# Running the first products of a two-layer block three units ahead of the second instead of two

## The chip, the cores and the metric

The kernel runs on one core of one Trainium2 chip. A core has TensorE (PE in the rows; its weight loads are PEld), VectorE (DVE), ScalarE (ACT), GpSimd (POOL) and SyncE (SP), which here only issues DMA. Each engine works through its own queue in order. The metric is device time in microseconds: 930.38 us, the median of three runs from 929.89 to 932.22.

## The reference

Three stages follow each other on 3072 tokens of width 512: attention in chunks of 32 with eight memory keys, a layer of 1024 with a softmax gate and a normalisation, and a last layer of 2048 with a leaky ReLU. The change touches only the last one:

```python
def _moe2_ref(x, w_in, w_out) -> np.ndarray:
    h = x @ w_in
    g = np.maximum(0.01 * h, h)
    return (g @ w_out).astype(np.float32)
```

Here `w_in` (512 x 2048) is W3 and `w_out` (2048 x 512) is W4. Both arrive as 64-bit floats.

## The kernel before

Every product is made from split operands: a value is held as a high and a low half (names ending in h and l, type fp32r), and each product is three matmuls, high by high, high by low, low by high. Raw 64-bit weights are turned into such halves on the chip. `load_raw` (line 92) fetches 128 x 512 of them, 512 KB, with one DMA from the queue of SP into a tile `raw`. `decode_steps` (line 100) then takes one ACT pass (line 107, from `raw` into `m`), four DVE passes (lines 109, 113, 117, 122), an ACT pass that writes the high half (line 129) and a subtraction that writes the low half (line 130; on DVE for W4). The pass of line 122 is the last that reads `raw`.

The tokens go in six blocks of 512. W3 is decoded while the earlier stages run and is parked in memory; `load_w3` (line 474) fetches it back in sixteen pieces, the first eight into `w3a`, the others into `w3b`. W4 is decoded in sixteen pieces during the first block, piece f + 1 being asked for just ahead of unit f.

In each block sixteen units run. `g_unit` (line 512) forms one 128 x 512 piece of the hidden layer: 12 matmuls of line 89 into a PSUM tile `gp` (four buffers), an ACT pass that scales it into `u` (line 518), a DVE maximum (line 519), a cast to the high half `gh` (line 523 on ACT in the first block, line 525 on DVE later) and a subtraction that gives the low half `gl` (line 526, on DVE in the first block, on POOL later). `o_unit` (line 531) multiplies that piece with the matching piece of W4: 12 matmuls of line 535 into four PSUM tiles `po`, three for each of four groups of 128 tokens, in the order gh by w4h, gh by w4l, gl by w4h. The main loop (line 561) puts each finished unit into a list `pend`, and `flush(n)` (line 552) emits `o_unit` for the oldest until n are left. So n says how many units the first products stand ahead of the second.

Just ahead of that loop the second layer's last four column groups are finished: `s_o` (line 338) forms them in the PSUM tile `x2p`, ACT copies each into `x2s` (line 351), which has a single buffer, and a DMA from ACT's queue carries it to `x2d` in memory (line 352). These copies and the first units of the last layer share ACT's queue.

Tiles come from pools that reuse the same memory: `dec2` (line 472) holds `raw` and `m` for W4, `pg` (line 506) holds `u`, `gh` and `gl`. A tile that is put where an older tile lay waits until that one is no longer used. A scheduler orders each engine's queue from the program and gives out the places in the pools.

Of the kernel before, what the change touches and what calls it, by code (L numbers as in the profile page):

```python
# [39 lines left out]
def tile_kernel(  # L40
# [425 lines left out]
    sb, sw3 = ExitStack(), ExitStack()  # L466
# [2 lines left out]
    w3hl = [w3p.tile([P, NF3, 2, KD, P], F32R, name="w3a")]  # L469
    ps_g = sw3.enter_context(tc.tile_pool(name="ps_g", bufs=4, space=PSUM, reuse_waits="tile"))  # L470

    dec2 = sw3.enter_context(tc.tile_pool(name="dec2", bufs=4, side="right", reuse_waits="tile"))

    def load_w3(f):
        w = w3hl[f // NF3][:, f % NF3].bitcast(F32)
        nc.sync.dma_start(out=w.rearrange("p h k f -> p (h k f)"), in_=w3d[f])

    x2e = w3p.tile([P, 2, KD, BT], F32R, name="x2e")
    def load_x(b):
        hl = x2o if b % 2 else x2e  # L480
        h, l = hl[:, 0], hl[:, 1]
        lf = l.bitcast(F32)
        nc.sync.dma_start(out=lf, in_=x2d[b])
        for kk in range(KD):
            nc.scalar.activation(h[:, kk], lf[:, kk], AF.Copy)
            (nc.vector if b < 2 else nc.gpsimd).tensor_tensor(
                out=l[:, kk], in0=lf[:, kk], in1=h[:, kk].bitcast(F32), op=ALU.subtract
            )
        return h, l
# [13 lines left out]
    w3hl.append(w4p.tile([P, KF2 - NF3, 2, KD, P], F32R, name="w3b"))  # L503
    x2o = w4p.tile([P, 2, KD, BT], F32R, name="x2o")
    pb = sb.enter_context(tc.tile_pool(name="pb", bufs=2, reuse_waits="tile"))
    pg = sb.enter_context(tc.tile_pool(name="pg", bufs=3, reuse_waits="tile"))
    ps_o = sb.enter_context(tc.tile_pool(name="ps_o", bufs=1, space=PSUM, reuse_waits="tile"))

    def load_w4(f):
        decode(load_raw(w4[f * P : (f + 1) * P, :], dec2), w4h[:, f], w4l[:, f], dec2, sub=nc.vector)  # L510

    def g_unit(b, f, xh, xl):
        ps = ps_g.tile([P, BT], F32, name="gp")
        w = w3hl[f // NF3][:, f % NF3]
        wh, wl = w[:, 0], w[:, 1]
        mm3(ps, [((wh[:, kk], wl[:, kk]), (xh[:, kk], xl[:, kk])) for kk in range(KD)])
        u = pg.tile([P, BT], F32, name="u")
        nc.scalar.activation(u, ps, AF.Copy, scale=0.01)  # L518
        nc.vector.tensor_tensor(out=u, in0=ps, in1=u, op=ALU.max)  # L519
        gh = pg.tile([P, BT], F32R, name="gh")  # L520
        gl = pg.tile([P, BT], F32R, name="gl")
        if b == 0:
            nc.scalar.activation(gh, u, AF.Copy)  # L523
        else:
            nc.vector.tensor_copy(gh, u)  # L525
        (nc.vector if b == 0 else nc.gpsimd).tensor_tensor(  # L526
            out=gl, in0=u, in1=gh.bitcast(F32), op=ALU.subtract
        )
        return gh, gl

    def o_unit(b, f, gh, gl, po):
        for t in range(TB):
            ts_ = slice(t * P, (t + 1) * P)
            for n, (a, w) in enumerate(((gh, w4h), (gh, w4l), (gl, w4h))):
                nc.tensor.matmul(  # L535
                    po[t], a[:, ts_], w[:, f],
                    start=(f == 0 and n == 0), stop=(f == KF2 - 1 and n == 2),
                )
        if f == KF2 - 1:
            for t in range(TB):  # L540
                late = b == NBLK - 1
                o = pg.tile([P, DM], F32, name="u") if late and t >= 2 else pb.tile([P, DM], F32, name="o")
                od = out[b * BT + t * P : b * BT + (t + 1) * P, :]
                if t % 2:
                    nc.vector.tensor_copy(o, po[t])
                else:
                    nc.scalar.activation(o, po[t], AF.Copy)
                (nc.scalar if late and t % 2 == 0 else nc.sync).dma_start(out=od, in_=o)
# [3 lines left out]
    def flush(n):  # L552
        while len(pend) > n:
            bb, ff, a1, a2 = pend.pop(0)
            if ff == 0:
                po[:] = [ps_o.tile([P, DM], F32, name=f"po{t}") for t in range(TB)]
            o_unit(bb, ff, a1, a2, po)
# [3 lines left out]
    for b in range(NBLK):  # L561
        xh, xl = nx
        for f in range(KF2):
            if b == 0:
                if f + LAG - 1 < KF2:
                    load_w3(f + LAG - 1)
                if f + 1 < KF2:
                    load_w4(f + 1)
            gh, gl = g_unit(b, f, xh, xl)
            pend.append((b, f, gh, gl))  # L570
            flush(2)
            if f == 8 and b + 1 < NBLK:
                nx = load_x(b + 1)
    flush(0)
# [49 lines left out]
```

## Time and profile before

| What | Value |
|---|---|
| Median of three runs | 930.38 us |
| Profiled execution | 930.47 us |
| Its span, first to last instruction | 928.7 us |
| PE busy | 890.5 us, 96% of the span |
| DVE, ACT, POOL busy | 48%, 34%, 19% |
| Mean granted TensorE clock | 0.996 |
| Last layer, start of its first product to the end of its last | 394.62 to 924.99 us |

Times inside the execution are microseconds from the first instruction. The profiled execution lasts 1.77 us longer than its span. The granted clock is a share of full speed: 1.00 is 2.4 GHz, 0.50 is 1.2 GHz.

### The profile page before, as it was taken

How to read it: one execution, taken by the hardware profiler on the slowest of the kernel's cores; microseconds unless marked ns; L12 is line 12 of the kernel's file. 1: busy time of each engine (PE TensorE's matmuls, PEld its weight loads, DVE VectorE, ACT ScalarE, POOL GpSimd, SP SyncE). 2: the span in 40 equal slices, each digit the busy share in tenths (PEclk: the TensorE clock that was granted, in tenths of full speed). 3: DMA queues.
4: the chain of work that ended last, by engine and by line, in shares of the span. 5: the costliest groups of instructions: out<-in, count | busy, mean ns of one | idle time of the engine just before them, and what ended most of it. 6: DMA issues, size and time to landing. Idle time of an engine off the chain costs nothing.

```text
span 928.7 us, 13605 instructions
## 1 busy us (share of the span) xinstructions
PE 890.5 (96%) x5248; PEld 714.8 (77%) x5248; DVE 450.1 (48%) x888; ACT 316.2 (34%) x830; POOL 172.9 (19%) x153
## 2 busy tenths in 40 slices
PE   3789999999999999989999999999999999999998
PEld 2467777777777768868888888888888888888886
DVE  4789976676787778279723112211221132112112
ACT  2477854455555555256421112111211121111111
POOL 2233310000000000000003224222422242222221
PEclk9999999999999999989999999999999999999999
DMA  9656685777888764886111001100200020001001
GB/s 221 170 168 202 183 235 183 223 245 203 253 240 254 209 194 170 329 296 248 45 47 46 1 1 45 46 1 1 80 12 1 1 91 1 0 1 46 1 1 46
DMA packets 51504, 109.94 MB, mean 118 GB/s; under 512 B 6640, under 2 KB 23024, under 8 KB 50672
## 3 DMA queue, kind: packets, MB, share of 16 engines
q1 hardware_dynamic: 38480, 93.87, 32.7%
q10 hardware_dynamic: 12960, 15.21, 5.2%
q8 instruction: 41, 0.67, 0.3%
q14 instruction: 23, 0.19, 0.1%
HBM read 79.70 MB, written 29.36 MB: 117 GB/s over the span
## 4 chain that ended last, share of the span: by engine, by line
PE 82%; DVE 8%; DMA 5%; ACT 2%; POOL 1%; issue 1%; SPq 0%; ACTq 0%; DVEq 0%; POOLq 0%
PE po L535 28%; PE gp L89 28%; PE x2p L345 13%; PE h L89 8%; DMA raw<-in_w 3%; PE att L240 2%; PE att L198 1%; DVE so L284 1%; PE tr L254 1%; ACT p L215 1%; DVE m L122 1%; POOL rstd L292 1%; PE tr L228 1%; DMA x2d<-x2s 1%; DVE hnm L276 1%
## 5 line engine op out<-in xcount | busy, mean ns | idle before, releaser
L519 DVE TENSOR_TENSOR u<-gp,u 128x512 f32<-128x512 f32 x96 | 66.3, 691 | 329.2 <-ACT u L518 329.2
L518 ACT ACTIVATE u<-gp 128x512 f32<-128x512 f32 x96 | 57.4, 598 | 370.5 <-PE gp L89 370.5
L526 POOL TENSOR_TENSOR gl<-u,gh 128x512 fp32r<-128x512 f32 x80 | 103.4, 1292 | 304.1 <-DVE gh L525 290.1
L535 PE MATMUL po<-w4h,gh 128*128 128x512 f32 x384 | 150.3, 391 | 3.3 <-ACT gh L523 3.1
L535 PE MATMUL po<-w4h,gl 128*128 128x512 f32 x384 | 150.5, 392 | 1.3 <-DVE gl L526 1.3
L535 PE MATMUL po<-w4l,gh 128*128 128x512 f32 x384 | 150.1, 391 | 0.0
L345 PE MATMUL x2p<-lhl,w2h 128*128 128x512 f32 x384 | 126.1, 404 | 2.3 <-ACT lhl L333 2.0
L535 PEld LDWEIGHTS po<-w4h,gh 128*128 128x128 f32 x384 | 72.5, 189 | 19.2 <-ACT gh L523 3.6
L535 PEld LDWEIGHTS po<-w4h,gl 128*128 128x128 f32 x384 | 72.6, 189 | 16.8 <-DVE gl L526 1.7
L345 PEld LDWEIGHTS x2p<-lhl,w2h 128*128 128x128 f32 x384 | 70.2, 188 | 19.2 <-ACT lhl L333 2.5
L535 PEld LDWEIGHTS po<-w4l,gh 128*128 128x128 f32 x384 | 72.5, 189 | 15.0
L345 PE MATMUL x2p<-lhl,w2l 128*128 128x512 f32 x192 | 77.7, 404 | 0.0
L89 PE MATMUL h<-w1l,xh 128*128 128x512 f32 x168 | 67.8, 404 | 1.9 <-POOL w1l L130 1.9
L89 PE MATMUL h<-w1h,xh 128*128 128x512 f32 x168 | 69.2, 412 | 0.5 <-ACT w1h L129 0.5
L89 PE MATMUL gp<-x2e,w3a 128*128 128x512 f32 x288 | 69.5, 391 | 0.0
L89 PE MATMUL gp<-x2o,w3a 128*128 128x512 f32 x288 | 69.2, 389 | 0.0
L89 PE MATMUL gp<-x2e,w3b 128*128 128x512 f32 x288 | 69.2, 389 | 0.0
L89 PE MATMUL gp<-x2o,w3b 128*128 128x512 f32 x288 | 69.2, 389 | 0.0
L89 PE MATMUL h<-w1h,xl 128*128 128x512 f32 x168 | 66.9, 398 | 0.0
L215 ACT ACTIVATE p<-att,nms 128x64 f32<-128x64 f32 x192 | 57.4, 320 | 22.8 <-DVE nms L208 22.6
L89 PEld LDWEIGHTS gp<-x2e,w3a 128*128 128x128 f32 x288 | 54.6, 190 | 11.5
L292 POOL TENSOR_TENSOR rstd<-ve,mhalf 128x1 f32<-128x1 f32 x24 | 15.9, 661 | 253.4 <-DVE ve L290 200.7
(107 smaller groups left out, 1259.8 us busy)
## 6 DMA issues: line engine op xcount, KB each, us to landing
raw<-in_w SPq DMA_DIRECT2D x48, 512.0 KB, 5.1
kbd<-in_kw SPq DMA_DIRECT2D x46, 256.0 KB, 4.6
vbd<-in_vw SPq DMA_DIRECT2D x46, 256.0 KB, 4.4
lnd<-sl SPq DMA_DIRECT2D x16, 512.0 KB, 3.8
lt<-lnd ACTq DMA_DIRECT2D x64, 128.0 KB, 4.4
q<-in_qt SPq DMA_DIRECT2D x24, 256.0 KB, 4.8
x2d<-x2s ACTq DMA_DIRECT2D x24, 256.0 KB, 3.9
out<-o SPq DMA_DIRECT2D x21, 256.0 KB, 2.0
```

Of the source, the lines that this page charges most:

```text
L89: nc.tensor.matmul(ps, a, b, start=(i == 0), stop=(i == 3 * n - 1))
L122: nc.vector.scalar_tensor_tensor(out=mu, in0=raw[:, :, 1], scalar=0x80000000, in1=mu, op0=ALU.bitwise_and, op1=ALU.bitwise_or,)
L198: nc.tensor.matmul(sc[cs, 2 * hp : 2 * hp + 2, :], q[:, hp, cs], k[:, :, hp, c, :], start=True, stop=True,)
L215: nc.scalar.activation(p[:, h], sc[:, h], AF.Exp, bias=nms[:, h : h + 1], scale=SCALE, accum_out=rs[:, h : h + 1],)
L228: nc.tensor.transpose(ptp[:, hp], p[:, 2 * hp : 2 * hp + 2].rearrange("p h k -> p (h k)"), ident)
L240: nc.tensor.matmul(xp[cs, 2 * hp : 2 * hp + 2, :], pt[:, hp, cs], v[:, :, hp, c, :], start=True, stop=True,)
L292: nc.gpsimd.tensor_tensor(out=rstd, in0=ve, in1=mhalf, op=ALU.pow)
L345: nc.tensor.matmul(ps, a[:, kk, es], r[:, kk], start=(kk == 0 and n == 0), stop=(kk == KF - 1 and n == 2),)
L518: nc.scalar.activation(u, ps, AF.Copy, scale=0.01)
L519: nc.vector.tensor_tensor(out=u, in0=ps, in1=u, op=ALU.max)
L526: (nc.vector if b == 0 else nc.gpsimd).tensor_tensor(out=gl, in0=u, in1=gh.bitcast(F32), op=ALU.subtract)
L535: nc.tensor.matmul(po[t], a[:, ts_], w[:, f], start=(f == 0 and n == 0), stop=(f == KF2 - 1 and n == 2),)
```

## The change

Three numbers change. `pg` gets four buffers each for `u`, `gh` and `gl` instead of three; `dec2` gets three each for `raw` and `m` instead of four; and the list is flushed down to three units instead of two. A buffer of `u`, `gh` and `gl` together takes 6 KB in each partition, and so does one of `raw` and `m`, so the space in total stays as it is, while the places inside it shift.

```diff
-    dec2 = sw3.enter_context(tc.tile_pool(name="dec2", bufs=4, side="right", reuse_waits="tile"))
+    dec2 = sw3.enter_context(tc.tile_pool(name="dec2", bufs=3, side="right", reuse_waits="tile"))
...
-    pg = sb.enter_context(tc.tile_pool(name="pg", bufs=3, reuse_waits="tile"))
+    pg = sb.enter_context(tc.tile_pool(name="pg", bufs=4, reuse_waits="tile"))
...
             gh, gl = g_unit(b, f, xh, xl)
             pend.append((b, f, gh, gl))
-            flush(2)
+            flush(3)
```

On PE, where the last layer begins (the rows with x2p are the end of the layer before it; `po` is numbered because it has four tiles), the difference reads:

```order
 L345 MATMUL x2p<-lhl,w2l 128x512
-L89 MATMUL gp<-x2e,w3a 128x512 x36
-L535 MATMUL po_4441<-w4h,gh 128x512
-L535 MATMUL po_4441<-w4l,gh 128x512
-L535 MATMUL po_4441<-w4h,gl 128x512
+L89 MATMUL gp<-x2e,w3a 128x512 x48
+L535 MATMUL po_4472<-w4h,gh 128x512
+L535 MATMUL po_4472<-w4l,gh 128x512
+L535 MATMUL po_4472<-w4h,gl 128x512
```

Twelve matmuls of a fourth unit now stand ahead of the first matmul on W4; from there on the two kinds alternate by twelve as they did, one unit further apart.

On DVE, at the same place, the first low half of an activation (line 526) reads in the difference:

```order
 L519 TENSOR_TENSOR u<-gp,u 128x512 [waits Activation_49]
-L526 TENSOR_TENSOR gl<-u,gh 128x512 [waits DMAHW3_49,DMAHW6_49,DMAHW2_49,Activation_49]
+L526 TENSOR_TENSOR gl<-u,gh 128x512 [waits Activation_49]
 L130 TENSOR_TENSOR w4l<-m,w4h 128x512 [waits Activation_49]
 L526 TENSOR_TENSOR gl<-u,gh 128x512 [waits Activation_49]
```

The three waits on DMAs that it loses are those of the transfers from `x2s` to `x2d`: in the kernel before, the first `gl` lies where `x2s` lay, and now the third `gh` does. On ACT's queue, with the tiles' numbers, before the change:

```order
L518 ACTIVATE u_4372<-gp_4359 128x512 [waits PE_49]
L107 ACTIVATE m_4413<-raw_4411 128x512 [waits DMAHW4_49]
L518 ACTIVATE u_4403<-gp_4390 128x512 [waits PE_49]
L523 ACTIVATE gh_4375<-u_4372 128x512 [waits DVE_49]
L129 ACTIVATE w4h_4325<-m_4382 128x512 [waits DVE_49]
L523 ACTIVATE gh_4406<-u_4403 128x512 [waits DVE_49]
L518 ACTIVATE u_4434<-gp_4421 128x512 [waits PE_49]
L107 ACTIVATE m_4460<-raw_4458 128x512 [waits DMAHW6_49,Activation_49]
L523 ACTIVATE gh_4437<-u_4434 128x512 [waits DVE_49]
```

and after it:

```order
L518 ACTIVATE u_4372<-gp_4359 128x512 [waits PE_49]
L107 ACTIVATE m_4413<-raw_4411 128x512 [waits DMAHW4_49,DVE_49]
L518 ACTIVATE u_4403<-gp_4390 128x512 [waits PE_49]
L523 ACTIVATE gh_4375<-u_4372 128x512 [waits DVE_49]
L129 ACTIVATE w4h_4325<-m_4382 128x512 [waits DVE_49]
L523 ACTIVATE gh_4406<-u_4403 128x512 [waits DVE_49,Pool_49]
L518 ACTIVATE u_4434<-gp_4421 128x512 [waits PE_49]
L107 ACTIVATE m_4444<-raw_4442 128x512 [waits DMAHW6_49,Activation_49]
L523 ACTIVATE gh_4437<-u_4434 128x512 [waits DMAHW3_49,DVE_49]
```

The order is the same; the pass on the fourth raw piece (`raw_4411`) also waits for DVE now, and the wait on the last transfer out of `x2s` (DMAHW3) has moved to the third `gh`. On SP's queue, the issues from the third raw piece of W4 on, before the change:

```order
L95 DMA raw_4380<-in_w4 128x1024 [waits DMAHW1_49,Pool_49]
L476 DMA w3a_4186<-w3d_62 128x1024 [waits DMAHW2_49]
L95 DMA raw_4411<-in_w4 128x1024 [waits DMAHW4_49]
L476 DMA w3a_4186<-w3d_62 128x1024 [waits DMAHW5_49]
L95 DMA raw_4458<-in_w4 128x1024 [waits DMAHW6_49,DVE_49,Activation_49]
```

and after it:

```order
L95 DMA raw_4380<-in_w4 128x1024 [waits DMAHW1_49]
L476 DMA w3a_4186<-w3d_62 128x1024 [waits DMAHW2_49]
L95 DMA raw_4411<-in_w4 128x1024 [waits DMAHW4_49,DVE_49,Activation_49]
L476 DMA w3a_4186<-w3d_62 128x1024 [waits DMAHW5_49]
L95 DMA raw_4442<-in_w4 128x1024 [waits DMAHW6_49,DMAHW7_49,DVE_49,Activation_49]
```

The fourth raw piece has no free buffer of its own any more: its issue waits for DVE's pass of line 122 on the first piece, and the issue of a W3 piece stands behind it.

## Rows read from the trace of the kernel before

**Rows 1.** The page, section 1 (busy us, share of the span, instructions)

```profile
PE 890.5 (96%) x5248; PEld 714.8 (77%) x5248; DVE 450.1 (48%) x888; ACT 316.2 (34%) x830; POOL 172.9 (19%) x153
```

**Rows 2.** Chain of waits, around the start and end of the last layer: start, us, what

```profile
394.62 5.46 PE gp L89 x24
...
400.71 6.27 DMA x2d<-x2s
...
407.93 4.63 PE po L535 x10
412.56 3.29 PE gp L89 x12
415.85 2.72 PE po L535 x12
...
916.82 8.17 PE po L535 x36
```

**Rows 3.** Timeline of PE, 394.4 to 408: start, us, what, idle and releaser

```profile
394.45 8.32 PE L89 MATMUL gp<-x2e,w3a 128*128 128x512 f32 x36
405.92 0.50 PE L535 MATMUL po<-w4h,gh 128*128 128x512 f32 x1 [3.14 <-ACT gh L523]
...
407.93 0.80 PE L535 MATMUL po<-w4h,gl 128*128 128x512 f32 x1 [1.28 <-DVE gl L526]
```

**Rows 4.** Stretches: length, busy PE PEld DVE ACT POOL, clock, DMA share, GB/s

```profile
330.00:335.00 5.00, 3.51 (x16) 2.56 (x14) 3.56 (x5) 1.81 (x6) 0.02 (x1) 1.00 0.90 273
...
406.00:407.00 1.00, 0.65 (x2) 0.21 (x2) 0.40 (x1) 1.00 (x3) 0.00 (x0) 0.87 0.98 395
413.00:414.00 1.00, 1.00 (x4) 0.79 (x4) 1.00 (x3) 0.15 (x1) 0.00 (x0) 0.71 0.40 57
424.00:434.00 10.00, 10.00 (x46) 8.29 (x45) 10.00 (x19) 6.83 (x13) 0.00 (x0) 1.00 0.96 383
454.00:464.00 10.00, 10.00 (x46) 8.29 (x45) 4.57 (x8) 3.03 (x5) 0.00 (x0) 1.00 0.00 0
```

**Rows 5.** Timeline of ACT, 394 to 406

```profile
394.50 0.33 ACTq L352 DMA_DIRECT2D x2d<-x2s  x1
...
400.08 0.60 ACT L351 ACTIVATE x2s<-x2p 128x512 f32<-128x512 f32 x1 [3.98 <-PE gp L89]
...
402.70 0.58 ACT L518 ACTIVATE u<-gp 128x512 f32<-128x512 f32 x1
403.17 0.66 ACT L107 ACTIVATE m<-raw 128x512 f32<-128x512 f32 x1
...
405.23 0.63 ACT L523 ACTIVATE gh<-u 128x512 fp32r<-128x512 f32 x1 [0.92 <-DVE u L519]
```

**Rows 6.** Timeline of DVE, 394 to 408

```profile
397.22 0.69 DVE L122 SCALAR_TENSOR_TENSOR m<-raw,m 128x512 uint32<-128x512 uint32 x1
...
404.52 0.68 DVE L519 TENSOR_TENSOR u<-gp,u 128x512 f32<-128x512 f32 x1
...
405.72 0.68 DVE L519 TENSOR_TENSOR u<-gp,u 128x512 f32<-128x512 f32 x1
407.18 0.69 DVE L526 TENSOR_TENSOR gl<-u,gh 128x512 fp32r<-128x512 f32 x1 [0.78 <-ACT gh L523]
```

**Rows 7.** Timeline of SP's queue, 394 to 424: issue, us of issuing, what

```profile
394.17 0.43 SPq L95 DMA_DIRECT2D raw<-in_w  x1
394.65 0.43 SPq L476 DMA_DIRECT2D w3a<-w3d  x1
...
400.99 0.37 SPq L95 DMA_DIRECT2D raw<-in_w  x1
...
420.54 0.33 SPq L95 DMA_DIRECT2D raw<-in_w  x1
```

**Rows 8.** Tile raw, its four issues from 393 to 411: us to landing

```profile
DMA to landing us min/median/max: 3.9/4.5/6.5
```

**Rows 9.** The page, section 6: issues, KB each, median us to landing

```profile
x2d<-x2s ACTq DMA_DIRECT2D x24, 256.0 KB, 3.9
```

## The prediction

> **What bounds the kernel now.** I read the page first: PE is busy for 890.5 of 928.7 us [rows 1], so only a gap of PE, or a stretch in which it runs slowly, can give time back. Next the chain of waits, for the last layer alone. From 412.56 on it is PE and nothing but PE, in pieces of twelve matmuls that take 2.72 us [rows 2]. The layer has 6 blocks of 16 units with two such pieces each, 192 pieces, so PE could do it in 192 x 2.72 = 522.24 us. It starts at 394.62 and ends at 916.82 + 8.17 = 924.99, 530.37 us later [rows 2]. So 8.13 us are lost somewhere. Nearly all of it is at the start: from 394.62 to the end of the sixth piece at 415.85 + 2.72 = 418.57 are 23.95 us, and six pieces are 16.32, which leaves 7.63 us [rows 2]. The other 0.50 us lies later, and I do not touch it.
>
> The timeline of PE shows the first part of the 7.63: after three units of W3 it stops at 402.77 and waits 3.14 us for the first `gh`, does two matmuls, and waits another 1.28 us for the first `gl` [rows 3]. That is 4.42 us. The stretches show the rest: the granted clock, 1.00 before, is 0.87 on average from 406 to 407 and 0.71 from 413 to 414 [rows 4]; ten matmuls from 407.93 take 4.63 us where twelve take 2.72, and the next twelve 3.29 [rows 2]. So PE runs at its lower level of 1.2 GHz for some six microseconds after it has stood idle, and this and the restart make the other 3.21 us.
>
> Last the timelines of the engines that PE waits for. ACT fills `x2s` at 400.08, which has one buffer and so needs the transfer that ACT issued at 394.50; it took until 400.0 [rows 5]. (The row names PE as the releaser, but a product of the next layer frees nothing there.) Behind it on ACT stand the first `u` at 402.70 and the first `gh` at 405.23 [rows 5]. The first `gl` on DVE is later still, at 407.18 [rows 6], because it lies where `x2s` lay and waits for the last transfer, 400.71 + 6.27 = 406.98 [rows 2].
>
> **The change, part by part.**
>
> *A fourth unit ahead.* Twelve matmuls move in front of the first product with W4. They add nothing in sum. PE then has work until 402.77 + 2.72 = 405.49. Its first matmul with W4 wants `gh` there, and the third wants `gl` two matmuls later, at 2 x 2.72 / 12 = 0.45 us more, 405.94.
>
> *The shifted buffers.* The first `gl` no longer waits for the transfer of 400.71. Everything else left as it was, `gh` is done at 405.23 + 0.63 = 405.86 [rows 5]. DVE comes free 0.60 us after it starts the second maximum (its passes of this size start that far apart, 404.52 to 405.72 for two), at 405.72 + 0.60 = 406.32, so `gl` runs from 406.32 to 407.01 [rows 6]. PE would wait 405.92 - 405.49 = 0.43 us and then about 407.05 - 406.37 = 0.68 us: 1.1 us in place of 4.42.
>
> *Three raw buffers.* The fourth raw piece was issued at 394.17. Now its issue waits for DVE's pass of 397.22, and goes out at 397.22 + 0.69, about 398.0 [rows 6], with the W3 piece of 394.65 behind it on SP's queue [rows 7]. This does two things of opposite sign.
>
> First, the transfer from `x2s` at 394.50 loses two rivals of 512 KB each for its first 3.5 us. It took 5.5 us before; the median of its 24 kind is 3.9 [rows 9]. At 3.9 it lands at 398.4, 1.6 us sooner, and the queue of ACT moves up with it: `u` from 402.70 to 401.1, the first maximum on DVE from 404.52 to 402.9. The Trainium skill ("DMA: Bandwidth & Descriptors", section "Issuing engines are not separate DMA queues") says that transfers issued by SP and by ACT run on the same sixteen engines and interleave, whoever issued them. By that rule the transfer gets quicker, as I take it; if ACT's transfers went their own way it would land at 400.0 still, and the 1.1 us above would stay. The trace agrees with the rule, in that 5.5 and 6.27 us were taken while other transfers ran, against a median of 3.9.
>
> Second, ACT's pass on that piece (403.17 before [rows 5]) now has a wait ahead of it, and the second `u` and the first `gh` stand behind it. Landings of `raw` in this stretch took 3.9 to 6.5 us, median 4.5 [rows 8], so the piece is there at 398.0 + 4.5 = 402.5 (401.9 to 404.5). At 402.5 the pass ends at 403.2, the second `u` at 403.7, the first `gh` at about 404.4; on DVE the second maximum runs from 404.1 to 404.8 and `gl` from there to 405.5. Both are ready before PE wants them, at 405.49 and 405.94: no wait, with 0.4 us to spare. At 6.5 everything from the pass on is 2 us later, `gl` ends at about 407.2, and PE waits some 1.2 us. So the cost of this part lies between 0 and 1.2 us at the start; I take 0, as the median landing does.
>
> *The clock.* With no gap, or with one of about 1 us, I expect no fall. From 330 to 335 PE stood idle for 1.49 of 5 us and the clock stayed at 1.00 [rows 4]; it fell after 3.14 and 1.28 us with only two matmuls between. So the 3.21 us go as well.
>
> *Later units.* Each unit now has six pieces, 16.3 us, from the end of its first product to the start of its second instead of four, 10.9 us, so a late `gh` or `gl` is covered better than before. At the end of the kernel three units stand after the last first product instead of two; that is the same work.
>
> **The sum.** The profiled execution took 930.47 us, 0.09 above the median of the three runs. 930.47 - 7.63 = 922.84, and against the median 922.75. I say 922.9.
>
> **Rivals.**
>
> *Part of the wait stays.* The transfer out of `x2s` is no quicker, or the raw piece lands late: 1.1 or 1.2 us as worked out, 924.0; up to about 3 us if both happen, 925.8. For it: DMA engines were busy at 0.96 to 0.98 of their time there [rows 4]. Against it: the later issues leave less in flight from 394 to 398.
>
> *The wait only moves.* If the fourth raw piece lands after about 407, 9 us after its issue, `gh` is as late as before plus one unit, the clock falls again, and the time is 926 to 930.4. Nothing in rows 8 comes near 9 us. That the change doesn't do what it says would give the same, 930.4; the order on PE shows that it does.
>
> *Slower: three raw buffers are too few for the rest of the first block.* One turn of a buffer, from an issue to the next issue into it, took 420.54 - 400.99 = 19.55 us with four buffers [rows 7], one piece each 4.9 us, while PE uses one in 5.44. If a turn stays that long with three, that is 6.5 us a piece. The fourth piece goes out at 398.0 and the sixteenth four turns later; it is decoded a turn after that, at 398.0 + 5 x 19.55 = 495.8. PE wants it at 405.49 + 15 x 5.44 = 487.1. PE then waits 8.7 us in that block, and if these waits bring the clock down once more, 3.2 on top: 922.84 + 11.9 = 934.7. It begins to cost at a turn of (487.1 - 398.0) / 5 = 17.8 us. Against it: the turn was long because DVE had four pieces in hand and worked without a break (10.00 of 10 us from 424 to 434), and it was through by about 459, some 30 us ahead of need (4.57 of 10 us from 454 to 464) [rows 4]; three in hand should turn round in about three quarters of that, 14.7 us. The Trainium skill ("Perfetto Trace Analysis", section "Optimization Strategy") warns that gaps which repeat on the engine that should be full can mean too few buffers for the next tile. It speaks against taking one away, and by it the time would be the one of this rival. The trace shows no repeating gap of PE in the first block with four buffers, and no run here yet with three.
>
> **How the numbers follow.** No wait left: 0.66, with 922.2 to 923.5 as its own range (it may also gain or lose some of the 0.50 us elsewhere). Part stays: 0.20, 923.5 to 926. Wait only moves, or nothing done: 0.08, 926 to 930.4. Slower: 0.06, about 934.7. A measurement of this kernel can tell 0.3%, 2.8 us, from no change, so faster means below 927.6: the first two cases and a third of the third, 0.88. Same 0.07, the rest of the third and the mildest of the fourth; slower 0.05. The range for 8 times in 10 is 922.0 to 926.0.
>
> **What would show it.** Right: 48 matmuls of W3 in one piece from 394.4 to about 405.5, the first product with W4 within 0.5 us behind them, a clock of 1.00 from 402 to 416, and 2.72 us for every piece; the first `x2s` wait on ACT ending near 398.5. Wrong: an idle row of PE above 1 us at 405.5 (with ACT's pass on `raw` waiting for a DMA it is the late landing; with `gl` waiting for `gh` alone it is ACT's queue), any idle of PE with W4 as releaser between 420 and 490, or a clock below 1.00 after 406.

## The result and the profile after

The changed kernel takes 921.13 us, the median of three runs (920.85, 921.13, 923.98), against 930.38 before: a ratio of 0.9908, with a 95% interval from 0.9881 to 0.9936. It is faster, by more than the 7.5 us forecast; 921.13 lies 0.9 us below the lower end of the predicted range. The same kernel run six more times in a later round gave a median of 922.87 and a ratio of 0.9921 (0.9896 to 0.9945). All nine runs together have their median at 922.74.

The profiled execution took 920.85 us with a span of 919.1 us and a mean granted clock of 1.00. Its page begins with this line (busy us, share of the span, instructions), which answers to [rows 1]:

```profile
PE 887.1 (97%) x5248; PEld 713.2 (78%) x5248; DVE 450.9 (49%) x888; ACT 315.8 (34%) x830; POOL 172.8 (19%) x153
```

The chain of waits through the last layer, as in [rows 2] (start, us, what):

```profile
393.10 10.88 PE gp L89 x48
403.98 2.72 PE po L535 x12
406.70 2.72 PE gp L89 x12
...
904.46 10.89 PE po L535 x48
```

The DMA, ACT and DVE pieces of [rows 2] are gone. The layer runs from 393.10 to 904.46 + 10.89 = 915.35, which is 522.25 us, or 192 pieces of 2.72 us: PE has nothing left to lose there. The timeline of PE says the same, with no idle time in front of the first product with W4, against 3.14 and 1.28 us in [rows 3]:

```profile
392.94 11.04 PE L89 MATMUL gp<-x2e,w3a 128*128 128x512 f32 x48
403.82 0.39 PE L535 MATMUL po<-w4h,gh 128*128 128x512 f32 x1
...
404.27 0.39 PE L535 MATMUL po<-w4h,gl 128*128 128x512 f32 x1
```

The stretches of [rows 4], in the trace after (busy PE, PEld, DVE, ACT, POOL; granted clock, DMA share, GB/s):

```profile
406.00:407.00 1.00, 1.00 (x7) 0.80 (x6) 1.00 (x3) 1.00 (x3) 0.00 (x0) 1.00 0.92 369
413.00:414.00 1.00, 1.00 (x6) 0.82 (x5) 1.00 (x3) 0.44 (x1) 0.00 (x0) 1.00 0.89 328
424.00:434.00 10.00, 10.00 (x46) 8.29 (x45) 8.05 (x15) 5.63 (x10) 0.00 (x0) 1.00 0.76 259
454.00:464.00 10.00, 10.00 (x46) 8.29 (x45) 4.62 (x8) 3.67 (x7) 0.00 (x0) 1.00 0.01 2
```

The clock stays at its upper level where it was 0.87 and 0.71, and DVE has slack from 424 to 434 where it had none.

Now the engines that PE waited for. The timelines of ACT, DVE and SP's queue answer to [rows 5 to 7]; subtract 392.94, the layer's start here, to compare with before, where it was 394.45. ACT:

```profile
392.44 0.33 ACTq L352 DMA_DIRECT2D x2d<-x2s  x1
...
396.84 0.60 ACT L351 ACTIVATE x2s<-x2p 128x512 f32<-128x512 f32 x1 [2.80 <-DMA x2d<-x2s]
...
400.80 0.68 ACT L107 ACTIVATE m<-raw 128x512 f32<-128x512 f32 x1 [0.76 <-DVE w4l L130]
401.38 0.57 ACT L518 ACTIVATE u<-gp 128x512 f32<-128x512 f32 x1
402.00 0.63 ACT L523 ACTIVATE gh<-u 128x512 fp32r<-128x512 f32 x1
```

DVE:

```profile
395.15 0.69 DVE L122 SCALAR_TENSOR_TENSOR m<-raw,m 128x512 uint32<-128x512 uint32 x1
...
403.08 0.68 DVE L526 TENSOR_TENSOR gl<-u,gh 128x512 fp32r<-128x512 f32 x1
```

SP's queue:

```profile
395.91 0.33 SPq L95 DMA_DIRECT2D raw<-in_w  x1
...
408.44 0.33 SPq L95 DMA_DIRECT2D raw<-in_w  x1
```

The transfer out of `x2s` that the first copy waits for takes 396.84 - 392.44 = 4.40 us from its issue to the next copy, against 400.08 - 394.50 = 5.58. The fourth raw piece goes out at 395.91, behind DVE's pass of 395.15, and nothing waits for its landing: ACT's pass on it waits 0.76 us for DVE. `gh` is done at 402.63 and `gl` at 403.77, ahead of PE's first matmuls that read them, at 403.82 and 404.27.

So the span became 9.6 us shorter. The layer accounts for 530.37 - 522.25 = 8.1 us. The other 1.5 us is outside: the layer starts at 393.10 on the chain instead of 394.62, in code that the change leaves alone. The chain of waits at the very start shows where that comes from. Before:

```profile
3.02 9.36 DMA raw<-in_w
12.40 13.58 DMA raw<-in_w
```

After:

```profile
3.01 8.45 DMA raw<-in_w
11.48 12.18 DMA raw<-in_w
```

These are two loads of raw weights, 512 KB each, one behind the other. The first is issued at the same moment in both; the second goes out from SP's queue as the first lands, at 12.40 and 11.48. They took 22.94 us together before and 20.63 after. Whether that is the change or the execution was the first question for the experiments.

### The profile page after: what moved, and what is told of

Same layout as the page of the kernel before. It is cut to its first block, busy times and chain, and to the rows that moved or that the text cites. A ratio compares the mean times of both kernels' runs of the same rounds, so it can differ in the third digit from the quotient of the medians.

```text
span 919.1 us, 13605 instructions
## 1 busy us (share of the span) xinstructions
PE 887.1 (97%) x5248; PEld 713.2 (78%) x5248; DVE 450.9 (49%) x888; ACT 315.8 (34%) x830; POOL 172.8 (19%) x153
## 4 chain that ended last, share of the span: by engine, by line
PE 85%; DVE 7%; DMA 3%; ACT 2%; POOL 1%; issue 1%; SPq 0%; ACTq 0%; DVEq 0%; POOLq 0%
PE po L535 28%; PE gp L89 28%; PE x2p L345 14%; PE h L89 9%; DMA raw<-in_w 2%; PE att L240 2%; PE att L198 1%; DVE so L284 1%; PE tr L254 1%; PE tr L228 1%; ACT p L215 1%; POOL rstd L292 1%; DVE hnm L276 1%; DVE m L122 1%; DVE nms L207 1%
## 5 line engine op out<-in xcount | busy, mean ns | idle before, releaser
L89 PEld LDWEIGHTS gp<-x2o,w3b 128*128 128x128 f32 x288 | 54.1, 188 | 11.2
```

Source lines behind the costliest of these rows:

```text
L89: nc.tensor.matmul(ps, a, b, start=(i == 0), stop=(i == 3 * n - 1))
```

## The experiments

Ten runs were made, each with a trace. The table puts these and the two of before and after side by side. S is the start of the first product of the last layer in PE's timeline. "Loads" is the sum of these two DMAs near the head of the program. "Copy" is the time from the issue of the transfer out of `x2s` near S to the next copy into `x2s`. "Idle" is PE's idle time ahead of its first products with W4. "Clock fell" says whether the granted clock fell in the layer. "Lost" is the time from S to the end of the last product, less the 522.4 us that the changed kernel took in its first profile.

| Trace | units ahead | raw buffers | first `gl` on x2s's place | S | loads | copy | idle: `gh`, `gl` | clock fell | lost |
|---|---|---|---|---|---|---|---|---|---|
| before | 2 | 4 | yes | 394.45 | 22.94 | 5.58 | 3.14, 1.28 | yes | 8.1 |
| after | 3 | 3 | no | 392.94 | 20.63 | 4.40 | none | no | 0 |
| e0_again | 3 | 3 | no | 394.74 | 23.05 | 4.66 | 0, 0.29 | no | 0.6 |
| e1_lag2 | 2 | 3 | no | 394.06 | 22.42 | 4.79 | 1.84, 0.40 | yes | 4.5 |
| e2_raw4 | 3 | 4 | no | 396.37 | 23.42 | 5.80 | 1.67, 0.41 | no | 2.8 |
| e3_swap | 3 | 3 | yes | 389.07 | 17.16 | 4.78 | none | no | 0.4 |
| e4_swap_before | 2 | 4 | no | 392.78 | 21.15 | 7.04 | 4.61, 0 | yes | 8.6 |
| e5_dec3 | 2 | 3 | yes | 393.45 | 20.83 | 4.68 | 2.18, 0.40 | yes | 4.7 |
| e6_dec2 | 3 | 2 | no | 392.46 | 20.87 | 3.43 | 1.92, 0 | no | 2.7 |
| e7_swap_b | 3 | 3 | yes | 392.27 | 20.58 | 4.50 | 0, 0.73 | no | 1.3 |
| e8_swap_c | 3 | 3 | yes | 393.61 | 21.29 | 4.61 | 0, 0.54 | no | 0.9 |
| e9_swap_d | 3 | 3 | yes | 393.98 | 22.29 | 4.35 | 0, 0.58 | no | 0.9 |

**The changed kernel once more (e0_again).** No edit.

> The changed kernel once more, to tell the share of the change from what differs between executions. The last layer lost 8.1 us before and 0.0 after, and it began 1.5 us sooner after, in code that the change leaves alone. Theory A (the 1.5 us come from the first loads and differ from run to run): the layer begins anywhere from 392.5 to 395 in this profile, and over five rounds the kernel is 8.1 us faster, a ratio of 0.9913. Theory B (they belong to the change): it begins near 393 again, and the ratio is 0.990 or below.

The median of six runs was 922.87 against 929.92. In this execution the two loads took 23.05 us and the layer began at 394.74, as late as before the change; it took 923.23 us in all. PE waited 0.29 us for `gl`. Four profiles of one kernel, e3_swap and its repeats below, differ more: loads from 17.16 to 22.29 us and starts from 389.07 to 393.98. Over the twelve traces S less the sum of the loads lies between 371.5 and 373.0, while the sum itself runs over 6.3 us. So the start of the layer follows these two DMAs, whatever the kernel is, and the 1.5 us of the first profile were the execution's and not the change's. Why the two loads take so differently long is not shown. The shortest case, from the chain of e3_swap:

```profile
3.02 7.06 DMA raw<-in_w
10.09 10.10 DMA raw<-in_w
```

**The unit ahead alone taken back (e1_lag2).**

```diff
-            flush(3)
+            flush(2)
```

> The changed kernel with the list flushed down to two units again; four buffers for the activation, three raw buffers and all places stay. Measured by what the last layer takes beyond 522.25 us, its 192 pieces of 2.72 (8.1 in the kernel before, 0.0 in the changed one). Theory A (the start-up gap is closed by three parts, the unit ahead being one): counted from the first matmul of the layer, PE runs out at 8.3 us, the first gh was done at 9.7 and the first gl at 10.8 in the changed kernel, so PE waits about 1.4 and 0.4 us and the layer loses 2.2 us with the clock staying at 1.00. Theory B (only the unit ahead counts): the gap of before is back, 7.6 us. Theory C (the unit ahead does nothing, the buffers did it): 0.

Median 926.37 of ten, ratio 0.9970 (0.9949 to 0.9991). The idle rows of PE's timeline:

```profile
404.23 0.50 PE L535 MATMUL po<-w4h,gh 128*128 128x512 f32 x1 [1.84 <-ACT gh L523]
405.36 0.50 PE L535 MATMUL po<-w4h,gl 128*128 128x512 f32 x1 [0.40 <-DVE gl L526]
```

The granted clock fell right behind them, in the stretches of the same trace:

```profile
406.00:407.00 1.00, 1.00 (x4) 0.79 (x3) 1.00 (x3) 0.48 (x1) 0.00 (x0) 0.56 1.04 311
```

Without the fourth unit 4.5 us are lost: 2.24 of idle time, as theory A had it, and the rest with the restart and a fall of the clock that theory A did not expect. By these two traces the smaller pool and the shifted places together give the other 8.1 - 4.5 = 3.6 us.

**Three raw buffers alone, in the kernel before (e5_dec3).**

```diff
-    dec2 = sw3.enter_context(tc.tile_pool(name="dec2", bufs=4, ...
+    dec2 = sw3.enter_context(tc.tile_pool(name="dec2", bufs=3, ...
```

> The kernel before with three raw buffers instead of four and nothing else: two units ahead, and the first gl still lies where x2s lay. Theory A: the fourth raw piece goes out later, the transfer out of x2s lands sooner, ACT's queue moves up 1.6 us; the first gh is ready 9.7 us after the start of the layer, but the first gl waits for the last transfer out of x2s until about 11.2, so PE waits 1.4 and then 1.6 us: 3.3 us lost if the clock stays, some 6 if it falls. Theory B (raw buffers only cost): 7.6 us or more, as before.

Median 926.67 of ten, ratio 0.9959 (0.9937 to 0.9981). The copy into `x2s` comes 4.68 us after the issue instead of 5.58, PE waits 2.18 us for `gh` and 0.40 for `gl`, and 4.7 us are lost:

```profile
403.96 0.50 PE L535 MATMUL po<-w4h,gh 128*128 128x512 f32 x1 [2.18 <-ACT gh L523]
405.09 0.79 PE L535 MATMUL po<-w4h,gl 128*128 128x512 f32 x1 [0.40 <-DVE gl L526]
```

The smaller pool by itself gains 8.1 - 4.7 = 3.4 us by the traces, and the interval of the ten times lies clear of 1. `gl` still lies where `x2s` lay, yet its wait, expected at 1.6 us, is as long as in e1_lag2, where it does not.

**The place of the first `gl` alone, in the kernel before (e4_swap_before).** The pool `pg` is opened ahead of `pb`, so that its tiles fall on other places.

```diff
-    pb = sb.enter_context(tc.tile_pool(name="pb", bufs=2, reuse_waits="tile"))
     pg = sb.enter_context(tc.tile_pool(name="pg", bufs=3, reuse_waits="tile"))
+    pb = sb.enter_context(tc.tile_pool(name="pb", bufs=2, reuse_waits="tile"))
```

> The kernel before with the two pools pg and pb taken in the other order and nothing else, which moves the first gl off the place of x2s (the second unit's gl comes to lie there). Theory A: the first gl runs at 406.3 instead of 407.18 on the clock of the trace before, 0.9 us sooner; the wait for gh (3.1 us) stays and with it the fall of the clock: 6.5 to 7 us lost at the start, and about 4 if the clock does not fall. Theory B (the place of gl is what counted): close to 0.

Median 929.0 of ten, ratio 1.0002 (0.9971 to 1.0033): no gain, to within 0.3%, some 3 us. `gl` no longer waits for the transfer, but `gh` still does, behind the copy on ACT's queue, and in this execution the copy came 7.04 us after the issue, 1.46 us later than before:

```profile
405.71 0.80 PE L535 MATMUL po<-w4h,gh 128*128 128x512 f32 x1 [4.61 <-ACT gh L523]
```

So the 8.6 us lost here do not price the place alone. Less the 1.46 us of the later copy they would be some 7.1, an estimate near theory A's 6.5 to 7.

**The place of `gl` put back in the changed kernel (e3_swap; the same kernel again in e7_swap_b, e8_swap_c and e9_swap_d).** The same swap of the two lines, in the changed kernel.

> The changed kernel with the two pools pg and pb taken in the other order and nothing else, which puts the first gl back where x2s lay. Theory A: with three units ahead and ACT's queue early, gl waits for the last transfer out of x2s only until about 11.1 us after the start of the layer, ends at 11.8, and PE wants it at 11.3: 0.6 us lost, clock 1.00. Theory B (the place of the first gl is the main part): 4 us or more lost.

Median 921.51 of ten (917.4 to 927.12), ratio 0.9923 (0.9893 to 0.9952), the same as e0_again to within the intervals. In its trace PE waits for nothing. Six of its ten runs had a mean clock of 0.996 to 0.999, though, while all nine of the changed kernel had 1.00, so three more profiles were taken of it.

> The kernel of e3_swap once more (the changed kernel with the first gl back on the place of x2s), for a second look at its last layer, since six of its ten executions had a mean granted clock below 1.00 and all nine of the changed kernel had 1.00. If the place of gl costs nothing that matters, the layer again lasts 522.4 to 523.5 us at a clock of 1.00 throughout, and a mean clock below 1.00 comes from a fall before the layer, near 336, as in e2_raw4. If it matters in those executions in which the last transfer out of x2s lands late, gl on DVE starts 11.5 us or more after the layer begins, PE shows an idle row of 0.5 to 2 us with gl as releaser, and the layer lasts 523.5 to 526 us, with the clock falling inside it.

> The same kernel, a third look, with the same two readings: 522.4 to 523.5 us for the layer with any fall of the clock lying before it, or 523.5 to 526 with a row of PE that waits 0.5 to 2 us for gl and the clock falling behind it.

> The same kernel, a fourth look, with the same two readings. If none of the three shows a mean clock below 1.00, the question stays open.

All three show a PE that waits for `gl`, by 0.73, 0.54 and 0.58 us, at a clock of 1.00 throughout; the layer lost 1.3, 0.9 and 0.9 us. From DVE's timeline in e8_swap_c, the transfer is what `gl` waits for:

```profile
404.90 0.69 DVE L526 TENSOR_TENSOR gl<-u,gh 128x512 fp32r<-128x512 f32 x1 [0.33 <-DMA x2d<-x2s]
```

Four traces with `gl` on that place lost 0.4 to 1.3 us, two without it 0 and 0.6. So the place is worth about half a microsecond once the rest of the wait is gone, an estimate from six traces that the times do not resolve. Where the clock fell in the six runs stays open, since none of the four profiled ones shows a fall.

**Four raw buffers kept, with the fourth unit (e2_raw4).** To make room, `u` has two buffers, and `gl` and `gh` are placed ahead of it; the output tile that shares the name `u` gets the same number.

```diff
-        decode(load_raw(w4[f * P : (f + 1) * P, :], dec2), ...
+        raw = dec2.tile([P, 512, 2], U32, name="raw", bufs=4)
+        nc.sync.dma_start(out=raw.rearrange("p f w -> p (f w)"), in_=w4[f * P : (f + 1) * P, :])
+        decode(raw, ...
...
-        u = pg.tile([P, BT], F32, name="u")
+        gl = pg.tile([P, BT], F32R, name="gl")
+        gh = pg.tile([P, BT], F32R, name="gh")
+        u = pg.tile([P, BT], F32, name="u", bufs=2)
...
-        gh = pg.tile([P, BT], F32R, name="gh")
-        gl = pg.tile([P, BT], F32R, name="gl")
```

> The changed kernel (three units ahead, four buffers of gh and gl) with four raw buffers; the room for it comes from u, which has two buffers; m keeps three, the first gl is off the place of x2s and the third gh on it, as in the changed kernel. The fourth raw piece is issued at once again. Theory A (the later issue speeds the transfer out of x2s and with it ACT's queue): ACT's queue is as late as in the kernel before, the first gl ends some 12.6 us after the start of the layer, and PE, which has work until 10.9, loses about 1.1 us, clock at 1.00. Theory B (raw buffers do not matter): 0 lost. Theory C (three raw buffers were a cost that the unit ahead outweighs): 0 lost and the decode ends sooner.

Median 924.73 of ten, ratio 0.9927 (0.9896 to 0.9959), which cannot be told from e0_again. The execution of the trace took 927.03 us, the second longest of the ten; in it 2.8 us are lost:

```profile
409.07 0.50 PE L537 MATMUL po<-w4h,gh 128*128 128x512 f32 x1 [1.67 <-ACT gh L525]
410.21 0.50 PE L537 MATMUL po<-w4h,gl 128*128 128x512 f32 x1 [0.41 <-DVE gl L528]
```

ACT's timeline says why. Two transfers out of `x2s` follow each other on one buffer:

```profile
390.66 0.33 ACTq L352 DMA_DIRECT2D x2d<-x2s  x1
...
396.81 0.60 ACT L351 ACTIVATE x2s<-x2p 128x512 f32<-128x512 f32 x1 [6.18 <-DMA x2d<-x2s]
397.44 0.33 ACTq L352 DMA_DIRECT2D x2d<-x2s  x1
...
403.24 0.60 ACT L351 ACTIVATE x2s<-x2p 128x512 f32<-128x512 f32 x1 [4.20 <-DMA x2d<-x2s]
```

The second is issued 1.07 us after S, where it was 0.05 in the kernel before, and takes 5.80. It is so late because the first went out late, at 390.66 or 5.71 us ahead of S, against 7.55 before; the first took no longer than in the kernel before (396.81 - 390.66 = 6.15 us to the next copy). This is one execution, so its 1.07 cannot be laid on the buffers.

**Two raw buffers (e6_dec2).**

```diff
-    dec2 = sw3.enter_context(tc.tile_pool(name="dec2", bufs=3, ...
+    dec2 = sw3.enter_context(tc.tile_pool(name="dec2", bufs=2, ...
```

> The changed kernel with two raw buffers instead of three, to see how near three are to too few. Turns of a raw buffer took 10 to 13.6 us with three. Theory A (a turn is mostly waiting in DVE's queue and shrinks with the buffers): a turn of about 10 us, 5.0 a piece against the 5.44 that PE uses, so no repeating gap; but ACT's passes on the third and fourth raw piece stand ahead of the first gh and wait for later transfers, which costs about 2 us at the start. Theory B (a turn has a floor of 12 us or more): 6 us a piece, PE waits again and again in the first block, 5 us or more in sum, and the clock may fall.

Median 923.24 of five, ratio 0.9933 (0.9905 to 0.9962). The copy comes soonest of all, after 3.43 us, but now ACT waits for the raw piece, and `gh` stands behind it:

```profile
400.73 0.66 ACT L107 ACTIVATE m<-raw 128x512 f32<-128x512 f32 x1 [1.42 <-DMA raw<-in_w]
404.19 0.66 ACT L107 ACTIVATE m<-raw 128x512 f32<-128x512 f32 x1 [2.81 <-DMA raw<-in_w]
404.76 0.61 ACT L523 ACTIVATE gh<-u 128x512 fp32r<-128x512 f32 x1
```

PE waits for it once:

```profile
405.43 0.50 PE L535 MATMUL po<-w4h,gh 128*128 128x512 f32 x1 [1.92 <-ACT gh L523]
```

That is its only idle row between 405 and 480. Two buffers still keep the whole first block fed.

## Why the prediction was right, and where it was wrong

*What bounds the kernel.* Right. The forecast counted 192 x 2.72 us for the layer and 8.13 us lost; after the change the layer takes 522.25 us and loses nothing.

*A fourth unit ahead.* Right, and the largest term. PE has work for 11.04 us from S, as forecast. Taken back alone (e1_lag2) it costs 4.5 us in the trace, and 3.5 between the medians (926.37 and 922.87).

*Three raw buffers.* Right in mechanism; that the size fits so well is partly luck. Forecast after S and measured: the `x2s` copy at 4.05 and 3.90, `gh` done at 9.95 and 9.69, `gl` at 11.05 and 10.83. But the transfer was to take 3.9 us from an issue at S + 0.05, and took 4.40 from an issue at S - 0.50. In e0_again it went out at S + 0.15 and took 4.66, and where the forecast had 0.4 us to spare PE waited 0.29. In the eight traces with three buffers the copy comes 4.35 to 4.79 us after the issue, against 5.58, 5.80 and 7.04 in the three with four, and 3.43 with two. The Trainium skill ("DMA: Bandwidth & Descriptors", section "Issuing engines are not separate DMA queues") states that transfers issued by different engines share the sixteen engines. The traces agree with it: fewer loads from SP at that moment, and the transfer from ACT is quicker. In the stretch from 1.55 to 3.55 us after S the share of the DMA engines' time that was busy fell from 0.93 to 0.47; before the change:

```profile
396.00:398.00 2.00, 2.00 (x10) 1.65 (x10) 1.90 (x4) 0.10 (x1) 0.00 (x0) 1.00 0.93 338
```

and after it:

```profile
394.50:396.50 2.00, 2.00 (x10) 1.66 (x9) 1.93 (x4) 0.00 (x0) 0.00 (x0) 1.00 0.47 180
```

What the smaller pool is worth is shown without the fourth unit (e5_dec3); beside it, it rests on the one trace of e2_raw4, since the times do not part the two kernels. The wait that was feared, ACT's pass on a late raw piece, did not come with three buffers and did with two. One wait was missed: `m` has three buffers as well, and the pass waits 0.76 us for DVE's subtraction on an earlier piece. The forecast had put a wait for the raw piece at that place, of about the same length, so the sum came out the same.

*The shifted buffers.* Mis-sized. They stood in the forecast as the reason that `gl`'s wait goes. Alone they gave nothing that the times show (e4_swap_before), because `gh`, behind the copies on ACT's queue, was late anyway. With three raw buffers and two units ahead PE waits 0.40 us for `gl` whether it lies on that place or not (e5_dec3 and e1_lag2, 4.7 and 4.5 lost). On top of the other two edits they give about 0.5 us.

*Part of the wait stays.* This rival was priced at 1.1 us if the transfer is no quicker. With four raw buffers and the fourth unit, 2.8 us stayed in the one trace. The price took the issue of that transfer as fixed at S + 0.05; it came anywhere from S - 0.50 (after) to S + 1.07 (e2_raw4), as the transfer ahead of it allowed.

*The clock.* The outcome was right, 1.00 in the whole layer, but the argument from 330 to 335 [rows 4] does not hold. There PE stood idle, for 2.04 us in all, since the wait runs on to 335.56, and the clock stayed; in e2_raw4, at the same place of the program, it fell. PE's idle rows there:

```profile
335.63 0.73 PE L345 MATMUL x2p<-lhl,w2h 128*128 128x512 f32 x2 [1.76 <-ACT lhl L333]
336.72 0.50 PE L345 MATMUL x2p<-lhl,w2h 128*128 128x512 f32 x1 [0.35 <-DVE lhl L334]
```

and the clock in the stretches behind them:

```profile
336.00:338.00 2.00, 1.65 (x6) 1.05 (x5) 1.97 (x5) 2.00 (x15) 0.00 (x0) 0.77 0.28 109
338.00:340.00 2.00, 2.00 (x8) 1.40 (x7) 1.31 (x4) 1.08 (x4) 0.00 (x0) 0.50 0.00 0
```

In e4_swap_before PE waited almost the same two times at that place, and the clock stayed at 1.00:

```profile
333.61 0.73 PE L345 MATMUL x2p<-lhl,w2h 128*128 128x512 f32 x2 [1.80 <-ACT lhl L333]
334.66 0.51 PE L345 MATMUL x2p<-lhl,w2h 128*128 128x512 f32 x1 [0.32 <-DVE lhl L334]
```

and the clock in its stretches:

```profile
334.00:336.00 2.00, 1.68 (x8) 1.12 (x7) 1.97 (x5) 2.00 (x15) 0.00 (x0) 1.00 0.27 102
336.00:338.00 2.00, 2.00 (x11) 1.51 (x11) 1.50 (x5) 1.11 (x4) 0.00 (x0) 1.00 0.00 0
```

The kernel after waits longer there, and its clock stayed at 1.00 for the whole execution:

```profile
334.07 1.22 PE L345 MATMUL x2p<-lhl,w2h 128*128 128x512 f32 x3 [2.79 <-ACT lhl L333]
```

*Slower, by too few raw buffers.* Fell. One turn of a buffer was 408.44 - 395.91 = 12.5 us with three, where the forecast said 14.7 and put the danger at 17.8. The rule that the forecast cited against the change is that of the Trainium skill ("Perfetto Trace Analysis", section "Optimization Strategy"): repeating gaps on the engine that should be full can mean too few buffers. The trace with three buffers shows no such gap, nor does the one with two.

*The sum: the step that failed.* The forecast took 7.63 us from one execution, "930.47 - 7.63 = 922.84", and left the rest of it as it was. Two parts of that rest moved. The first is the start of the layer, 1.52 us sooner in the profile after, and this varies by itself: from 389.07 to 396.37 over the twelve traces, with the two loads near the head of the program. The forecast put this term at nothing, and a range that begins at 922.0 has no room for it, though the three runs before already lay 2.3 us apart. With the start as late as before, 920.85 + 1.52 = 922.37. The second is the 0.50 us "I do not touch". In the kernel before, the chain of waits leads at the end of the first block through a DMA out of `o` to a PE that waits:

```profile
489.29 2.73 PE gp L89 x12
...
494.58 4.20 DMA out<-o
...
498.91 0.70 DVE o L545
...
499.65 0.96 PE po L535 x3
500.62 2.73 PE gp L89 x12
```

Three pieces of PE lie between 492.02 and 500.62, 8.60 us where three times 2.72 are 8.16, so this wait and its restart are 0.44 of the 0.50. After the change the layer's pieces leave no room for such a wait. The fourth unit is not needed for that: in e1_lag2 and e5_dec3, still two units ahead, PE has no idle row there either, and in e4_swap_before it waits 0.51 us. What decides it there is not shown. Without the two, 920.85 + 1.52 + 0.50 = 922.87, which is the forecast. That the median of the six later runs is the same figure is luck, but all six, from 921.84 to 923.46, lie around the forecast. The 7.63 us were sized right, but for the 0.6 that e0_again still lost; what failed is that the rest of one execution was taken to repeat.

## What to carry to other kernels

Before a sum is made against one execution, ask what of it repeats: here the head of the program moves the whole by several microseconds, more than the last edits on a tuned kernel give, and a range has to hold that spread beside the unknown costs of the change. When two things are late for one engine, price each edit by the one that is late after the others; the wait with the plainest label, `gl` on a transfer, was worth about half a microsecond of the eight, by six traces. A buffer taken from a pool can gain time, since it holds back loads that compete with a transfer on which the next stage waits.

## What the runs showed of the hardware that was not expected

Two loads of 512 KB near the head of the program, the first issued at 3.0 us in every trace and the second as the first lands, took from 17.16 to 23.42 us together on the same instructions beside other loads, and the start of the last layer follows them.

The length of a gap did not tell whether the granted clock falls. It fell to 0.50 behind idle times of 1.84 and 0.40 us (e1_lag2), 2.18 and 0.40 (e5_dec3), and 1.76 and 0.35 (e2_raw4, near 336); it stayed at 1.00 behind 1.67 and 0.41 (e2_raw4, near 409), 1.80 and 0.32 (e4_swap_before, near 334), 1.92 (e6_dec2) and 2.79 (after, at 334.07). The closest pair, 1.76 and 0.35 against 1.80 and 0.32, stands at the same place of the program. What decides is not shown.
